# Seven early query loads split by head pair instead of by partition half, with their order mended in the matmul reads and a new plan of steps

One NeuronCore (core 0) of one Trainium2 chip runs the kernel. The metric is the device time of one launch in microseconds (us), the median of the fast runs; a "ratio" is the mean time of one kernel's fast runs over that of the other's fast runs of the same rounds, so it is not quite the ratio of the medians quoted beside it.

## The reference

Decayed linear attention in blocks of 64 (batch 4, 8 heads, 768 positions, 64 wide), then an MLP with a sine in it (512 to 2048 to 512) on the 3072 tokens.

```python
intra = einsum('bhic,bhjc->bhij', qb, kb) * Dmask[None]
intra = einsum('bhij,bhjd->bhid', intra, vb)
inter = einsum('bhid,bhde->bhie', qb * lam_pow[None], kv_state)
out[:, :, sl] = intra + inter
kv_state = lam_block[None, :, None, None] * kv_state + einsum('bhsd,bhse->bhde', kb_dec, vb)
# then, with x = the attention's output as [3072, 512]:
h = x @ w_in
s = sin(alpha * h)
g = h + s * s / (alpha + 1e-09)
return g @ w_out
```

## The kernel before

The attention is cut into 24 units of 4 heads and 256 positions. Four units make a group of 512 tokens, and the MLP of a group needs its four units. Queries, keys and values of a unit are loaded (256 KB each), cast to bf16, queries and keys are turned (in nine units by TensorE, with a copy out of PSUM after it, in the other 15 by a DMA), and then come scores, mask, inter and output. For units 1 to 7 (`Q4`) the queries travel with four neighbouring rows in one run of 1 KB:

```python
def load(op, u, i, gate):
    ...
    if i == 0 and u in Q4:
        for x in reversed(range(2)):                  # one issue per half of the partitions
            op.ins = SY.dma_start(
                out=tl[half[x]].rearrange("p h two e -> p (h two e)")
                .rearrange("p (g y) -> p g y", g=2),
                in_=src[2 * x:2 * x + 2].rearrange("g (p j) e -> p g (j e)", j=4))
            ...
def turn_ev(op, tr, u, j):                            # PSUM -> SBUF, after the turn
    o, i = T[u, "qt"][:, j], tr.tile[:]
    if j == 0 and u in Q4:                            # puts the positions in order
        o = o.rearrange("q par hp (p a) -> q a (par hp) p", a=2)
        i = i.rearrange("q a x i -> q a (x i)").rearrange("q a (y p) -> q a y p", y=4)
    (A.copy or V.tensor_copy)(out=o, in_=i)           # shortened
```

All steps are operations with an assumed duration and a priority (the table `TUNE`). A small planner simulates them once, at build time, and from that fixes the order in which each engine gets its instructions. On the chip every engine then works through its list in that order. If a step's data are late, the steps behind it wait too.

## Time and profile before

| | before |
|---|---|
| time | 219.86 us (219.25 to 219.96, 3 runs) |
| span of the profiled run, granted clock | 218.1 us, 1.00 |
| TensorE busy | 205.9 us, 94% |
| first matmul of the MLP | at 22.34 us |
| query loads of units 1 to 4 issued | at 2.33, 4.97, 7.67 and 10.41 us |
| TensorE idle from 34.3 to 214 us | 2.46 us |

It is read from the start: TensorE is full from the first MLP matmul to the end, so what delays that matmul should delay the end, and what keeps it waiting is the loads. The lines are in the prediction.

### The profile page before, as it was taken

What the parts mean: (1) busy time and instruction counts of PE and PEld (TensorE: products, weight loads), DVE (VectorE), ACT (ScalarE), POOL (GpSimd) and SP (SyncE); (2) the same over time, 40 slices, a digit from 0 to 9 for tenths busy, and PEclk for the clock granted to TensorE, in tenths of its full rate; (3) what the DMA queues carried; (4) which work ended last, traced back from release to release, by engine and by line L of the source; (5) the groups of instructions that cost most, each with busy time, mean ns of one, the idle gap of its engine ahead of it and who ended that gap; (6) DMA issues with size and microseconds to landing.
All of it is one profiled execution on the core that took longest, in us unless ns stands there. A gap on an engine that the chain in (4) does not pass through costs nothing.

```text
span 218.1 us, 5252 instructions
## 1 busy us (share of the span) xinstructions
PE 205.9 (94%) x2042; PEld 105.1 (48%) x2070; DVE 124.6 (57%) x203; ACT 140.4 (64%) x253; POOL 122.8 (56%) x201
## 2 busy tenths in 40 slices
PE   8786999999999999999999999999999999999992
PEld 3354544455536554455645545445445444444461
DVE  3678686537659973477767864738625643543000
ACT  4374698575499754876948778558726877775111
POOL 4569699948999999988899591313111001030000
PEclk9999999999999999999999999999999999999999
DMA  5999999998999992899999992202222022111253
GB/s 168 254 256 217 207 200 215 259 255 233 291 174 181 298 314 64 174 263 195 290 219 223 298 186 49 48 3 50 48 51 48 2 51 48 28 37 35 48 120 72
DMA packets 60460, 33.65 MB, mean 154 GB/s; under 512 B 18051, under 2 KB 57491, under 8 KB 60435
## 3 DMA queue, kind: packets, MB, share of 16 engines
q1 hardware_dynamic: 56096, 29.04, 59.1%
q0 software_dynamic: 4224, 4.19, 11.7%
q8 instruction: 16, 0.26, 0.5%
q10 hardware_dynamic: 114, 0.07, 0.1%
q14 instruction: 10, 0.07, 0.1%
HBM read 27.27 MB, written 6.29 MB: 154 GB/s over the span
## 4 chain that ended last, share of the span: by engine, by line
PE 70%; DMA 13%; POOL 6%; ACT 4%; issue 3%; SPq 2%; DVE 1%; POOLq 0%; ACTq 0%; DVEq 0%
PE ops L962 30%; PE hps L926 28%; DMA st_v<-in_v_dram 7%; DMA st_k<-in_k_dram 6%; PE okv L962 3%; PE sp L773 2%; PE okv L896 2%; SPq L698 2%; ACT s L933 2%; POOL qk L717 2%; PE okv L883 1%; POOL vb L723 1%; DVE gall L945 1%; ACT s L940 1%; POOL s L942 1%
## 5 line engine op out<-in xcount | busy, mean ns | idle before, releaser
L945 DVE SCALAR_TENSOR_TENSOR gall<-s,r_sb,hps 128x512 bf16<-128x512 bf16 (+1 forms) x97 | 70.1, 740 | 55.0 <-ACT s L940 33.9
L926 PE MATMUL hps<-xt,w_in_sb 128*128 128x512 bf16 (+1 forms) x371 | 90.6, 377 | 1.9 <-DVE gall L945 0.5
L933 ACT ACTIVATE s<-hps,alpha_sb 128x512 bf16<-128x512 f32 (+1 forms) x97 | 64.6, 679 | 34.4 <-PE hps L926 31.1
L962 PE MATMUL ops<-w_out_sb,gall 128*128 128x512 bf16 (+1 forms) x358 | 81.6, 370 | 1.0 <-issue 0.6
L962 PEld LDWEIGHTS <-gall 128*128 128x128 bf16 x400 | 38.3, 98 | 41.4
L926 PEld LDWEIGHTS <-w_in_sb 128*128 128x128 bf16 x388 | 36.7, 98 | 44.3 <-issue 2.7
L942 POOL TENSOR_TENSOR s<-s 128x512 bf16<-128x512 bf16 x24 | 24.8, 1041 | 39.7 <-ACT s L933 39.6
L940 ACT ACTIVATE s<-s 128x512 bf16<-128x512 bf16 (+1 forms) x73 | 44.5, 623 | 1.4
L782 DVE TENSOR_TENSOR sm<-sp,mask 128x512 bf16<-128x512 f32 x48 | 32.6, 684 | 6.1 <-PE sp L773 6.1
L723 POOL TENSOR_TENSOR vb<-st_v,R 128x512 bf16<-128x512 f32 x24 | 25.0, 1045 | 8.6 <-DMA st_v<-in_v_dram 6.2
L968 ACT COPY ob<-ops 128x512 f32<-128x512 f32 x21 | 12.2, 582 | 19.1 <-PE ops L962 18.9
L832 POOL TENSOR_TENSOR kvx<-kva,kvs 128x128 f32<-128x128 f32 x32 | 14.6, 457 | 14.8 <-ACT kva L817 14.5
L835 POOL TENSOR_TENSOR kvbd<-kvx,LBD 128x256 bf16<-128x256 f32 x32 | 19.6, 614 | 2.5
L913 DVE TENSOR_TENSOR xt<-okv,ET 128x512 bf16<-128x512 f32 x24 | 16.5, 686 | 3.5 <-PE okv L896 3.5
L999 PE MATMUL bz<-const-bfloat16-1.0 128*128 128x256 bf16 (+1 forms) x35 | 9.6, 343 | 1.7 <-PEq L1335 0.8
L717 POOL CAST qk<-st_q 128x512 bf16<-128x512 f32 x16 | 9.6, 614 | 1.4 <-PE okv L807 1.4
L773 PE MATMUL sp<-qt 64*64 64x128 bf16 x384 | 10.0, 221 | 0.0
L717 POOL CAST qk<-st_k 128x512 bf16<-128x512 f32 x16 | 9.7, 615 | 0.0
L896 PE MATMUL okv<-sm,vb 64*64 64x128 bf16 x384 | 9.7, 218 | 0.0
L873 POOL TENSOR_TENSOR kvs<-kvx,ET 128x128 f32<-128x128 f32 x24 | 9.5, 405 | 0.0
L883 PEld LDWEIGHTS <-kvbd 128*128 128x128 bf16 x80 | 6.2, 98 | 5.6 <-POOL kvbd L835 1.1
L883 PE MATMUL okv<-qt,kvbd 128*128 128x128 bf16 x80 | 8.6, 219 | 0.3 <-POOL kvbd L835 0.3
(64 smaller groups left out, 104.4 us busy)
## 6 DMA issues: line engine op xcount, KB each, us to landing
st_k<-in_k_dram SPq DMA_DIRECT2D x24, 256.0 KB, 5.2
st_v<-in_v_dram SPq DMA_DIRECT2D x24, 256.0 KB, 4.9
out_dram<-ob SPq DMA_DIRECT2D x46, 128.0 KB, 2.4
st_q<-in_q_dram SPq DMA_DIRECT2D x17, 256.0 KB, 5.2
w_out_sb<-in_moe_w_out_dram POOLq DMA_DIRECT2D x4, 512.0 KB, 14.4
st_q<-in_q_dram SPq DMA_DIRECT2D x14, 128.0 KB, 5.6
w_in_sb<-in_moe_w_in_dram POOLq DMA_DIRECT2D x2, 512.0 KB, 7.8
w_in_sb<-in_moe_w_in_dram POOLq DMA_DIRECT2D x1, 768.0 KB, 10.6
```

The costliest lines, as they stand in the source:

```text
L717: ENGINE[op.eng].tensor_copy(out=o, in_=i)
L723: ENGINE[op.eng].tensor_tensor(out=T[u, "vb"][:], in0=T[u, "v"][:].rearrange("p h two e -> p two h e"), in1=R[:, :, hs].unsqueeze(3).to_br ...
L782: V.tensor_tensor(out=T[u, "sm"][:, hd], in0=T[u, "sp"][hd][:], in1=mask[:].unsqueeze(2).to_broadcast([P, 2, 2, P]), op=ALU.mult)
L835: G.tensor_tensor(out=bd[:], in0=X.unsqueeze(2).to_broadcast([P, 2, 2, D]), in1=LBD[:, hs, :].unsqueeze(3).to_broadcast([P, 2, 2, D]), op= ...
L883: nc.tensor.matmul(out=okv[:, c, hp * P:(hp + 1) * P], lhsT=sts[c][:, hp].rearrange("p two e -> p (two e)"), rhs=T[u, "qt"][:, 0, :, hp, h ...
L913: V.tensor_tensor(out=xt[g][:, 2 * hh:2 * hh + 2, bb, :, :].rearrange("p hp c i -> p c hp i"), in0=T[u, "op"][:, :, 0:2 * P].rearrange("p ...
L926: op.ins = nc.tensor.matmul(out=op.tile[:, cols], lhsT=w_in_sb[:, c, f * P:(f + 1) * P], rhs=xt[g][:, c].rearrange("p b c i -> p (b c i)") ...
L933: A.activation(out=op.tile[:, cols], in_=mm.tile[:, cols], func=ACTF.Sin, scale=alpha_sb[:, f:f + 1])
L940: A.activation(out=op.tile[:, cols], in_=s1, func=ACTF.Square)
L942: ENGINE[op.eng].tensor_tensor(out=op.tile[:, cols], in0=s1, in1=s1, op=ALU.mult)
L945: V.scalar_tensor_tensor(out=gall[g][:, f, cols], in0=sq.tile[:, cols], scalar=r_sb[:, f:f + 1], in1=mm.tile[:, cols], op0=ALU.mult, op1=A ...
L962: op.ins = nc.tensor.matmul(out=first.tile[:, cols], lhsT=gall[g][:, f, m * P:(m + 1) * P], rhs=w_out_sb[:, f, cols], start=(f == 0), stop ...
```

## The change

The intent: each of the two issues of a query load should cover all 128 partitions, not 64; the copy out of PSUM becomes plain, and the order of the positions is put right by the access pattern with which scores and inter read the queries. The plan was made anew for that.

```diff
-            for x in reversed(range(2)):
-                op.ins = SY.dma_start(
-                    out=tl[half[x]].rearrange("p h two e -> p (h two e)")
-                    .rearrange("p (g y) -> p g y", g=2),
-                    in_=src[2 * x:2 * x + 2].rearrange("g (p j) e -> p g (j e)", j=4))
...
+            for g in range(2):
+                ins = SY.dma_start(
+                    out=tl[:].rearrange("p h two e -> p (h two e)")[:, g * 4 * D:(g + 1) * 4 * D],
+                    in_=src.rearrange("(s g) (p j) e -> g s p (j e)", g=2, j=4)[g])
...
-        o, i = T[u, "qt"][:, j], tr.tile[:]
-        if j == 0 and u in Q4:
-            ...
+            V.tensor_copy(out=T[u, "qt"][:, j], in_=tr.tile[:])
...
+    def queries(u, rows, hp, c):
+        Q = T[u, "qt"][rows, 0]
+        if u not in Q4:
+            return Q[:, :, hp, half[c]]
+        Q = Q.rearrange("q y x i -> q (y x i)").rearrange(
+            "q (a two x p) -> q two x p a", a=2, two=2, x=2)
+        return Q[:, :, hp, 32 * c:32 * c + 32, :]
...
-                            rhs=QT[half[hd], 0, :, hp, half[c]],
+                            rhs=queries(u, half[hd], hp, c),
...
-    BEGIN, LAND, DEPTH = {"SP": 0.4, "POOL": 2.0}, 1.7, 6
+    BEGIN, LAND, DEPTH = {"SP": 0.4, "POOL": 2.0}, 1.55, 6
... (967 of the 973 priorities of TUNE new, 31 steps with another engine or none prescribed)
```

The bytes land in the same places before and after. Only the cut between the two issues differs.

## The prediction

> **What bounds the kernel now.** I read the page's header and tenths first, then the table of stretches, then the chain that ended last in its early part, then the rows of the DMA issues, then the instructions that touch the query tile.
>
> ```profile
> span 218.1 us, 5252 instructions
> PE 205.9 (94%) x2042; PEld 105.1 (48%) x2070; DVE 124.6 (57%) x203; ACT 140.4 (64%) x253; POOL 122.8 (56%) x201
> ```
>
> TensorE is the bound by share. But the share is an average, so the next view splits it (columns: stretch, its length, then busy time and count of PE, PEld, DVE, ACT, POOL, granted clock, DMA share, GB/s).
>
> ```profile
> 15.00:20.00 5.00, 3.64 (x89) 2.40 (x90) 4.42 (x8) 2.73 (x6) 4.97 (x8) 1.00 1.28 230
> 22.40:34.30 11.90, 11.26 (x98) 5.23 (x99) 8.77 (x15) 10.14 (x20) 9.57 (x18) 1.00 1.21 204
> 34.30:60.00 25.70, 24.96 (x300) 13.06 (x305) 15.38 (x25) 15.86 (x32) 21.25 (x34) 1.00 1.09 254
> 60.00:100.00 40.00, 39.24 (x461) 20.31 (x465) 26.37 (x40) 30.14 (x53) 37.93 (x63) 1.00 0.97 209
> 100.00:140.00 40.00, 39.46 (x433) 20.52 (x429) 29.30 (x44) 29.42 (x53) 29.48 (x49) 1.00 0.89 196
> 140.00:180.00 40.00, 39.74 (x317) 19.57 (x320) 21.47 (x31) 26.29 (x45) 6.69 (x10) 1.00 0.16 34
> 180.00:214.00 34.00, 33.84 (x172) 16.82 (x172) 9.06 (x13) 17.09 (x29) 3.08 (x3) 1.00 0.23 51
> ```
>
> From 34.3 us to 214 us TensorE stands idle for 0.74 + 0.76 + 0.54 + 0.26 + 0.16 = 2.46 us. So what a new schedule can still win there is about 2.5 us, and the rest of the time is matmuls that the change does not touch. The other place with slack is the start: the first feed-forward matmul of the MLP runs at 22.3 us, and what the chain shows before it is loads:
>
> ```profile
> 1.78 4.83 DMA st_v<-in_v_dram
> 6.63 4.91 DMA st_k<-in_k_dram
> 11.76 7.27 DMA st_k<-in_k_dram
> 19.06 0.63 ACT qk L715
> 19.73 0.41 PE pt L743 x4
> 20.17 0.60 ACT qt L753
> 20.80 0.28 PE bz L999
> ```
>
> Three loads in a row make 17 of the first 19 us; the last takes 7.27 us from issue to landing for 256 KB, so it stood in a queue. The start is a matter of the transfers, with POOL (4.97 of 5 us busy from 15 to 20) close behind. These are the rows of the loads (KB each, median us to landing):
>
> ```profile
> st_k<-in_k_dram SPq DMA_DIRECT2D x24, 256.0 KB, 5.2
> st_q<-in_q_dram SPq DMA_DIRECT2D x17, 256.0 KB, 5.2
> st_q<-in_q_dram SPq DMA_DIRECT2D x14, 128.0 KB, 5.6
> ```
>
> The 14 issues of 128 KB are the seven query loads that the change touches: half the bytes, yet no sooner there. Last, the evacuation of the turned queries and keys, DVE and then ACT (min/median/max ns):
>
> ```profile
> L755 DVE COPY qt<-pt x10: 415/425/734, 4.9 to 52.7; 128x512 bf16<-128x512 bf16 x10
> L753 ACT COPY qt<-pt x8: 586/666/773, 9.0 to 55.6; 128x512 bf16<-128x512 bf16 x8
> ```
>
> One shape, two durations on each engine: the long ones (0.73) write the early queries in a permuted order with a gap between neighbours, the short ones (0.42 and 0.59) are plain.
>
> **What the Trainium skill says.** (1) "SBUF — State Buffer", Door 1, the DMA port swizzle: partitions 0..63 reach 8 of the 16 DMA ports, so a transfer on 64 partitions gets about half the rate of one on 128. The trace leans that way: in the microsecond from 3 to 4, with key and value loads on 128 partitions, 0.31 MB moved (309 GB/s); from 4 to 5 and 6 to 7, with the split query loads among them, 0.22 MB each (224 and 217 GB/s). It doesn't separate them cleanly. (2) "DMA: Bandwidth & Descriptors", Why a DMA increments its semaphore by 16 and not by 1: the number of engines is the largest k up to 16 that divides the slowest dimension of both access patterns. In the kernel before that dimension is 64 or 128 on both sides, so 16 engines; no load in the trace has a small outer dimension, so nothing here tests it. (3) "SBUF — State Buffer", same section, the note on 16-byte cachelines: a read that goes to a new line at every element pays a penalty. No matmul of the trace reads its moving operand that way, so this is open too. (4) "VectorE: DVE Perf Modes", What auto-detection actually checks: two results per cycle need 16-bit operands at unit step. That agrees with 0.42 against 0.73 us on DVE, though ACT too loses 0.14.
>
> **The change part by part.**
>
> Query loads, units 1 to 7. Before: two issues, one to each half of the partitions (64 x two runs of 1 KB). After: two issues, each to all 128 partitions (one run of 1 KB). Same bytes, same place of every byte, same number of issues. If the rate of these goes from some 220 to some 310 GB/s (the windows above), units 1 to 3 (0.79 MB) save 0.79/220 - 0.79/310, about 1.0 us of transfer. POOL and the casts stand beside it, so I let 0.4 us reach the first MLP matmul. There is a hazard: the new source pattern goes head pair (2), then 64 row groups, then a run. Its slowest dimension is 2 and cannot be merged with the 64. By the rule (2) such a transfer would use 2 engines, not 16. That is the first rival below.
>
> Evacuation. Permuting copies become plain: 0.31 us less on DVE, 0.14 on ACT, seven times, so 1 to 2.2 us of engine time. Neither engine bounds; on the path lies about one of them in the start: 0.2 us.
>
> Matmuls. The order is now made where scores (16 matmuls per unit) and inter (2 matmuls in units 1 to 3, 4 in units 4 to 7) read the queries; neighbours of a run lie 512 bytes apart. The chain gives 0.22 us for 4 inter matmuls, 0.054 each, and 0.35 us for 16 scores, four of which run side by side. If such a read runs at half rate, a unit pays 4 x 0.054 = 0.21 us for scores and 0.054 for each inter. Units 4 to 7 lie at 47 to 59 us, where TensorE is full: 4 x 0.21 + 16 x 0.054 = 1.7 us more. Units 1 to 3 lie where TensorE runs filler, so most of theirs is hidden. At about even odds of the penalty, I count 0.8 us.
>
> Plan. The priorities of all steps are new; the landing time assumed is 1.55 instead of 1.7 us. Squares pinned to ACT go from 65 to 70, to POOL from 22 to 20. No instruction is added or removed. Slack to win: the 2.46 us above, and 22.4 to 34.3, where 38 full and 8 half matmuls of the first MLP layer (38 x 0.216 + 8 x 0.108 = 9.1 us) and about 0.8 us of attention fill 11.9 us: 2 us. A plan adapted to cheaper evacuations should find perhaps a quarter of the 4.5 us: 1.0 us.
>
> Sum: -0.4 - 0.2 + 0.8 - 1.0 = -0.8 us, so 219.1 us where the loads run as meant.
>
> **The rivals.**
>
> First, the loads fall onto 2 engines. Then each of those carries 128 KB of a unit's queries. In the 3 to 4 us window an engine moved 309/16 = 19 GB/s; 1 KB runs may reach 25 (an estimate), so 5 to 7 us per unit, plus its share of keys and values (32 KB, 1.7 us). A unit's loads would then take 7 to 8 us on these engines, where the trace has q1 to q4 issued 2.7 us apart. Units 1 to 3 would be there at about 26 us instead of 17 to 19, the first full MLP matmul would go from 24.3 to about 31, and the span would grow by 5 to 8 us: 225 to 228. Units 4 to 7 are mostly covered by the 128 first-group matmuls. For it: the rule is stated plainly, and nothing in the new pattern escapes it. Against it: whoever planned this anew shortened the landing time, the opposite of what such loads would have shown, and left the assumed query transfer as it was. I give it one in four.
>
> Second, nothing reaches the end: the earlier data wait for POOL (values to scale, weight issues, 4.97 of 5 us), the slow reads eat the rest, and the plan is only different: 219.5 to 220.8. For it: POOL is full from 15 to 20, and the windows after 34.3 are at 97 to 99%. I give it a third.
>
> Third, the new plan removes most of the idle time of 22 to 60 us: 2.5 to 3 us, 217. Against it: the plan before was tuned too. For over 2% (below 215.5) it would need nearly all the 4.5 us; that I give one in twenty.
>
> **Range and chances.** The middle of the meant branch is 219.1 with a spread of about 1.2; the 2-engine branch at 225 to 228 has a quarter of the weight and moves the median up a little: 219.2 us. One case in ten below 217.2, one in ten above 226.0. Faster by over 2%: 0.05; within: 0.71; slower (above 224.3): 0.24.
>
> **What would show it.** In the DMA issues, the 128 KB query row should land in clearly less than 5.6 us if the ports were the matter, and in more, with the tenths of DMA sinking in the first 25 us, if engines are lost. The copies to qt should be uniformly 0.42 and 0.59. The scores and inter matmuls of units 1 to 7 should show by their group times (0.35 per 16, 0.22 per 4) whether the read pays. The first MLP matmul should come at 21.5 to 22.5 us, or near 28 in the rival. TensorE's idle time from 34.3 to 214 should shrink from 2.46 us if the plan earned anything. The prediction is wrong if the loads lose their engines, if the permuted read costs far more than half rate, or if the plan stalls a later group of units.

## The result

The changed kernel takes **254.95 us** (254.53 to 255.34, 4 runs) against 219.71 us (the kernel before with a fourth run; the table above has three); ratio 1.1606, 95% interval 1.1575 to 1.1637. That is 35 us slower, outside the range of the prediction. The page of the changed kernel, its header, its tenths and its loads:

```profile
span 252.9 us, 5273 instructions
PE 219.4 (87%) x2070; PEld 111.4 (44%) x2070; DVE 122.8 (49%) x201; ACT 142.2 (56%) x256; POOL 121.7 (48%) x200
...
PE   8274612899966899999999999999999999999993
...
PEclk9955575599997799999999999999999999999998
DMA  4336496299346995999996899523311030111233
```

A slice is 6.3 us here. In the first 16 slices (some 100 us) TensorE has holes, its clock falls to half in some of them, and the DMA engines are mostly idle in a start that was bound by transfers before. From slice 17 on TensorE is at 9 again, up to the last slice.

What the DMA engines did in two stretches of the start comes next (the third number from the end is the clock, then the DMA share and GB/s). First the changed kernel:

```profile
10.50:12.00 1.50, 0.00 (x0) 0.00 (x0) 0.00 (x0) 0.00 (x0) 0.03 (x1) 0.99 0.14 45
10.00:15.00 5.00, 2.15 (x13) 1.60 (x14) 0.00 (x0) 2.38 (x4) 1.57 (x2) 0.70 0.19 59
```

Then the kernel before:

```profile
10.00:15.00 5.00, 3.99 (x97) 2.14 (x96) 3.25 (x8) 3.18 (x10) 2.99 (x4) 1.00 1.20 263
```

Two of 16 engines are a share of 0.125. In the first stretch the share is 0.14, at 45 GB/s: two engines at some 22 GB/s each. The trace's DMA packets, counted one by one, agree: two are under way in 79% of that stretch, three or four in the rest, never fewer than two. (65 of these 103 packets have 512 bytes, the size of the runs of keys and values: their share on the two engines waits there as well.) Before, from 10 to 15 us, at least 16 packets were under way at any time (a share over 1 means that transfers overlapped in an engine), at 263 GB/s. This is the first rival of the prediction.

The issues show the same from the other side (start, duration; two issues per line). The kernel before, then the changed one from its first query load by head pair:

```profile
4.97 1.26 SPq L690 DMA_DIRECT2D st_q<-in_q_dram  x2
7.67 1.26 SPq L690 DMA_DIRECT2D st_q<-in_q_dram  x2
10.41 1.26 SPq L690 DMA_DIRECT2D st_q<-in_q_dram  x2
```

```profile
2.32 1.47 SPq L689 DMA_DIRECT2D st_q<-in_q_dram  x2
7.89 3.95 SPq L689 DMA_DIRECT2D st_q<-in_q_dram  x2
15.31 3.90 SPq L689 DMA_DIRECT2D st_q<-in_q_dram  x2
22.35 3.98 SPq L689 DMA_DIRECT2D st_q<-in_q_dram  x2
```

The distance of neighbouring units from unit 2 on is 7.0 to 7.4 us, not 2.7. The work fits: 128 KB of queries on each of the two engines at 22 GB/s is 6.0 us, and their share of keys and values (32 KB) 1.5. The issuing got slower too, 3.9 us a pair and not 1.26, so the keys and values behind it are issued late as well. But the first pair, which met no such load ahead of it, took 1.47 us (1.41 in the kernel before), and the pair at 56.18 us, after a pause, 1.18: issuing was slow only behind loads that were not done.

The chain that ended last, in the changed kernel up to the first MLP matmul:

```profile
16.65 9.78 DMA st_q<-in_q_dram
26.43 17.52 DMA st_k<-in_k_dram
...
43.97 0.63 ACT qk L712
...
44.64 0.61 PE pt L740 x4
...
46.83 1.01 PE hps L927 x4
```

The last matmul is the first of the MLP. In the kernel before it stands here:

```profile
22.34 0.61 PE L926 MATMUL hps<-xt,w_in_sb 128*128 128x256 bf16 x4
```

It comes at 46.83 us and not 22.34, so 24.5 of the 35 us are lost there. These four matmuls take 1.01 us and not 0.61, at a granted clock of 0.52 from 40 to 50 us and 1.00 before: a part of the loss lies in matmuls that run, but slowly. And the load it waits for is the keys of unit 4. But the first group consists of units 0 to 3. Its MLP doesn't need unit 4 at all. A second hole lies between 60 and 100 us, where TensorE is idle for 5.4 us and the clock is at 0.91 to 0.92. From the first MLP matmul to the end the changed kernel takes 206.1 us, the kernel before 195.8: these are the other 10.3 us.

### The profile page after: what moved, and what is told of

Its sections match the earlier page's. It is cut to its first block, busy times and chain, and to the rows that moved or that the text cites. A ratio compares the mean times of both kernels' runs of the same rounds, so it can differ in the third digit from the quotient of the medians.

```text
span 252.9 us, 5273 instructions
## 1 busy us (share of the span) xinstructions
PE 219.4 (87%) x2070; PEld 111.4 (44%) x2070; DVE 122.8 (49%) x201; ACT 142.2 (56%) x256; POOL 121.7 (48%) x200
## 4 chain that ended last, share of the span: by engine, by line
PE 66%; DMA 18%; SPq 7%; POOL 4%; ACT 1%; DVE 1%; issue 1%; POOLq 0%; ACTq 0%; DVEq 0%
PE ops L963 30%; PE hps L927 27%; DMA st_q<-in_q_dram 8%; DMA st_k<-in_k_dram 7%; SPq L695 4%; SPq L689 3%; DMA st_v<-in_v_dram 3%; PE sp L774 3%; PE okv L897 2%; PE okv L884 2%; POOL s L943 1%; DVE gall L946 1%; PE okv L808 1%; PE bz L1000 1%; POOL kvbd L836 1%
## 5 line engine op out<-in xcount | busy, mean ns | idle before, releaser
L963 PE MATMUL ops<-w_out_sb,gall 128*128 128x512 bf16 (+1 forms) x368 | 85.0, 377 | 0.0
L927 PEld LDWEIGHTS <-w_in_sb 128*128 128x128 bf16 x388 | 37.3, 98 | 45.6 <-issue 3.0
L941 ACT ACTIVATE s<-s 128x512 bf16<-128x512 bf16 (+1 forms) x74 | 45.4, 623 | 1.6
L943 POOL TENSOR_TENSOR s<-s 128x512 bf16<-128x512 bf16 x23 | 23.8, 1041 | 34.4 <-ACT s L934 34.3
L733 PE MATMUL pt<-iden,qk 128*128 128x128 bf16 x28 | 3.6, 270 | 24.3 <-ACT qk L712 20.2
L712 ACT CAST qk<-st_q 128x512 bf16<-128x512 f32 x8 | 4.9, 615 | 31.8 <-DMA st_q<-in_q_dram 31.8
L733 PEld LDWEIGHTS <-qk 128*128 128x128 bf16 x28 | 2.2, 116 | 25.8 <-ACT qk L712 25.3
L1000 PE MATMUL bz<-const-bfloat16-1.0 128*128 128x256 bf16 (+1 forms) x35 | 12.4, 423 | 1.2 <-PEq L1336 0.8
L774 PE MATMUL sp<-qt 64*64 64x128 bf16 x384 | 11.9, 241 | 0.1
L897 PE MATMUL okv<-sm,vb 64*64 64x128 bf16 x384 | 10.8, 237 | 0.0
```

Of the source, the lines that this page charges most:

```text
L774: nc.tensor.matmul(out=T[u, "sp"][hd][half[c], par, hp, :], lhsT=QT[half[hd], 1, par, hp, half[c]], rhs=queries(u, half[hd], hp, c), start ...
L927: op.ins = nc.tensor.matmul(out=op.tile[:, cols], lhsT=w_in_sb[:, c, f * P:(f + 1) * P], rhs=xt[g][:, c].rearrange("p b c i -> p (b c i)") ...
L941: A.activation(out=op.tile[:, cols], in_=s1, func=ACTF.Square)
L943: ENGINE[op.eng].tensor_tensor(out=op.tile[:, cols], in0=s1, in1=s1, op=ALU.mult)
L963: op.ins = nc.tensor.matmul(out=first.tile[:, cols], lhsT=gall[g][:, f, m * P:(m + 1) * P], rhs=w_out_sb[:, f, cols], start=(f == 0), stop ...
```

## The experiments

All twelve results are correct against the reference. Times are medians of the fast runs, 4 to 6 of each but for unit 4 alone, which had two fast runs (228.41 and 228.59) and two slow ones (231.89 and 232.09, at the same clock). One slow run each fell to the loads by halves (228.57) and the interleaved pairs (223.82). The kernel before had 219.3 to 219.8 us in these rounds. The record gives chip 8 for eight of the runs and chip 4 for four (the two cuts of the halves and the two with unit 4's work moved back), each set with the kernel before beside it.

| run | time us | ratio to before | 95% interval |
|---|---|---|---|
| changed, loads by halves | 221.33 | 1.0079 | 1.0023 to 1.0135 |
| before, loads by head pair | 254.17 | 1.1578 | 1.1520 to 1.1636 |
| changed, pairs interleaved | 220.18 | 1.0027 | 0.9984 to 1.0070 |
| changed, loads by halves, old data path | 220.76 | 1.0040 | 0.9995 to 1.0084 |
| halves cut 62 + 2 | 255.56 | 1.1630 | 1.1574 to 1.1687 |
| halves cut 56 + 8 | 221.18 | 1.0070 | 1.0006 to 1.0133 |
| head pair for units 1 to 3 only | 235.47 | 1.0714 | 1.0653 to 1.0775 |
| head pair for unit 4 only | 228.50 | 1.0404 | 1.0331 to 1.0478 |
| head pair for units 5 to 7 only | 231.57 | 1.0546 | 1.0493 to 1.0598 |
| unit 4 by head pair, its work moved back | 242.88 | 1.1032 | 1.0960 to 1.1103 |
| the same with loads by halves (control) | 240.48 | 1.0934 | 1.0875 to 1.0993 |
| before, pairs interleaved | 217.90 | 0.9928 | 0.9883 to 0.9973 |

**The loads alone, taken out and put in.** Theory: the source pattern begins with a dimension of 2, so each load runs on two DMA engines. Rivals: the new plan stalls, or the permuted reads of the matmuls are slow.

```diff
 # changed kernel, loads by halves
-            for g in range(2):  ...  "(s g) (p j) e -> g s p (j e)"
+            for x in reversed(range(2)):  ...  "g (p j) e -> p g (j e)"
```

> The changed kernel with one thing undone: the query loads of units 1 to 7 are again one issue per half of the partitions (slowest source dimension 64), bytes in the same places; new plan, plain copies and permuted matmul reads stay. Engine theory (a source whose slowest dimension is 2 runs on 2 DMA engines): all of the 35 us come from the loads, so this lands at 218 to 222 us and the 128 KB loads of queries land within 7 us. Plan theory (the new priorities put TensorE's queue in an order that stalls): stays above 240. Read theory (the permuted moving operand is what is slow): stays above 235, with scores of units 1 to 7 at twice 0.35 us or more.

It took 221.33 us. Of the 35 us, 33.6 (254.95 less 221.33) are gone with the loads.

```diff
 # kernel before, loads by head pair
-            for x in reversed(range(2)):  ...  "g (p j) e -> p g (j e)"
+            for g in range(2):  ...  "(s g) (p j) e -> g s p (j e)"
```

> The kernel before with one thing added: the query loads split by head pair, everything else as it was (plan, permuting copies, plain reads). Engine theory: 245 to 260 us, with the same gaps of about 7 us between the issues of neighbouring units. Plan theory: below 225. Read theory: below 225, since no read is permuted here.

It took 254.17 us, with issues at 8.17, 15.68 and 22.75 us: the whole loss, with the old plan and plain reads. So the new plan and the permuted reads are out as its cause.

**Engines, or the order of the source?** Two experiments, from both sides. First, the same coverage (one head of each pair, all 128 partitions, one run of 1 KB each), but with the row groups outermost:

```diff
-                    in_=src.rearrange("(s g) (p j) e -> g s p (j e)", g=2, j=4)[g])
+                    in_=src.rearrange("(s g) (p j) e -> g p s (j e)", g=2, j=4)[g])
...
-            "q (a two x p) -> q two x p a", a=2, two=2, x=2)
+            "q (a two p x) -> q two x p a", a=2, two=2, x=2)
```

> The changed kernel with the pairs interleaved over the partitions: each load still takes one head of each pair and covers all 128 partitions with one run of 1 KB each, but partition 2p+pair instead of 64 pair+p, so the slowest source dimension is 64 and not 2. Same bytes, same number of issues, same heads. Engine theory: 217 to 221 us, query loads landing in at most 5.6 us; if the ports of the partitions matter too, 0.3 to 1 us faster than the version with loads by halves. Rival (it is the reading of two head pairs at once, or one run per partition on all 128, that is slow, not the number of engines): stays above 240.

It took 220.18 us, and the 128 KB query loads land in 4.7 us (median). Swapping two letters in the pattern, with the reads adapted, undoes the loss. Second, the opposite: the old order, but each half's 64 partitions cut so that the divisor rule, point (2) of the prediction, gives two engines, or 14 and 8.

```diff
+                for lo, hi in ((0, 62), (62, D)):     # control: 56
+                    ins = SY.dma_start(
+                        out=tl[x * D + lo:x * D + hi]...,
+                        in_=src[2 * x:2 * x + 2].rearrange("g (p j) e -> p g (j e)", j=4)[lo:hi])
```

> The changed kernel with loads by halves, but each half's 64 partitions cut into 62 and 2: four issues per unit, source order rows first as in the kernel before, no head pair outermost. By the divisor rule of the Trainium skill 62 shares with the numbers up to 16 only the divisor 2, so both pieces run on 2 engines. If the number of engines is the cause: 245 to 260 us, like the changed kernel, though nothing of its source order is left. If the order of the head pairs in the source is the cause: 219 to 226.

> The control for the cut into 62 and 2: the same four issues per unit, cut into 56 and 8, which the rule gives 14 and 8 engines. Expected: 220 to 226 us; what it loses against loads by halves (221.5) is the price of two more issues per unit. If this one is slow too (over 240), the number of issues is the cause and not the engines.

The cut at 62 took 255.56 us, the cut at 56 took 221.18. Both have four issues per unit; six partitions more or less decide over 34 us. The stretch of the 62 run shows the two engines again:

```profile
10.50:12.00 1.50, 0.00 (x0) 0.00 (x0) 0.00 (x0) 0.00 (x0) 0.42 (x1) 0.50 0.14 46
```

In its packets two are under way in 81% of this stretch, again never fewer. This settles it: the loss follows the number of engines, and that follows the common divisor of the slowest dimensions, as the Trainium skill says ("DMA: Bandwidth & Descriptors", Why a DMA increments its semaphore by 16 and not by 1). Only the two engines were counted; that the control ran on just 14 and 8 is not shown.

**Where the 33.6 us fall.** Now only some units use the split by head pair (`if u in (1, 2, 3):` and so on, the others load by halves).

> The changed kernel with the split by head pair kept for units 1 to 3 only; units 4 to 7 load by halves. It gives the part of the loss that units 1 to 3 make. If every late load counts where it falls: values of unit 3 land at about 30 us as in the changed kernel, the first matmul of the MLP runs at 33 to 36 us instead of 21.3, and the time is 231 to 234 us. If the start is hidden by later slack: below 226.

> The changed kernel with the split by head pair for unit 4 only. Unit 4 belongs to the second group, which the first MLP matmuls don't need. If TensorE's fixed order makes them wait (unit 4's transposes stand ahead of them in its queue): first MLP matmul 3 to 6 us later than 21.3, time 223 to 227 us. If only data count: no change against loads by halves, 219.5 to 222 us.

> The changed kernel with the split by head pair for units 5 to 7 only, which are loaded after the start. In the changed kernel TensorE stood idle about 5.5 us between 60 and 100 us at a lower clock. Expected: start as with loads by halves (first MLP matmul at about 21.3 us), a gap before the second group's scores, time 226 to 231 us. My recorded prediction had these covered by the first group's 128 matmuls: then 220 to 223.

Against loads by halves (221.33) they cost 14.1, 7.2 and 10.2 us. The sum, 31.5, is all but 2 us of the 33.6: the parts nearly add up. Unit 4's part is the least certain: it rests on two fast runs, and its two slow ones would make it 10.6 to 10.8. The first MLP matmul comes at 37.06 us for units 1 to 3, at 27.96 for unit 4 and at 21.23 for units 5 to 7, where the gap lies later. All three came out above what was expected (for the time of units 5 to 7 by half a microsecond): none of the three losses is covered by other work as a whole.

**Why should unit 4 cost anything?** In the run with unit 4 only, TensorE's line shows it (start, duration, and in brackets what it waited for):

```profile
22.16 0.61 PE L743 MATMUL pt<-iden,qk 128*128 128x128 bf16 x4 [2.84 <-ACT qk L722]
...
22.77 0.45 PE L894 MATMUL okv<-qt,kvbd 128*128 128x128 bf16 x2
...
25.77 0.61 PE L750 MATMUL pt<-iden,qk 128*128 128x128 bf16 x4 [1.76 <-ACT qk L722]
...
27.96 1.01 PE L937 MATMUL hps<-xt,w_in_sb 128*128 128x256 bf16 x4
```

The `pt` matmuls turn unit 4's queries and keys. They stand in the queue before the inter and output matmuls of the first group's units, and those before the MLP. To test this, I made the plan put unit 4's query cast and value scaling after the fifth MLP tile. The edit does not hold back its key cast. It also lets the loads of the output weights wait for unit 3's value scaling and not for unit 4's. This ran once with unit 4 by head pair and once, as control, with all loads by halves:

```diff
+    u4 = {o.name: o for o in plan.ops}
+    for x in ("cq4", "sv4"):
+        u4[x].after.append(f1_mm[0, 4])
-    WH = (4, 4, 4, 4)
+    WH = (3, 3, 3, 3)
```

> Unit 4 on loads by head pair as in the run with unit 4 only (230.2 us), but the plan puts unit 4's casts, its value scaling and with them its transposes behind the first five MLP tiles of the first group. If the loss of that run is TensorE and POOL waiting in their own order for data that the next work doesn't need: at most 3 us above its control, and the first MLP matmul at about 22 us. If the late data themselves or the crowded engines cost the time: 7 us or more above the control.

> The control: the same altered plan with all loads by halves. 219 to 224 us; its own distance from the run with loads by halves (221.5) is the price of the altered order and says nothing of the loads.

The first MLP matmul of the run with unit 4 by head pair:

```profile
21.79 0.61 PE L937 MATMUL hps<-xt,w_in_sb 128*128 128x256 bf16 x4 [1.00 <-DMA w_in_sb<-in_moe_w_in_dram]
```

It no longer waits for unit 4: 21.79 us and not 27.96, and its control has 22.05. That the late load stopped this matmul only through the order of the steps is shown. The size of what is saved is not. The altered plan is itself bad: the control takes 240.48 us and not the 219 to 224 that I expected of it, with TensorE idle for 5.7 us from 60 to 80 us at a clock of 0.74. The distance of the two runs is 2.4 us instead of 7.2, but a plan with that much slack may hide the rest. A version that moved unit 4's steps in the finished order deadlocked in simulation, by my account alone: it was not run. So no run separates this further.

**The permuted reads, the copies, the plan.** The changed kernel with loads by halves and, in addition, the permuting copies and plain reads of the kernel before:

```diff
-                            rhs=queries(u, half[hd], hp, c),
+                            rhs=QT[half[hd], 0, :, hp, half[c]],
 # and turn_ev as in the kernel before
```

> The changed kernel's plan alone: loads by halves, permuting copies and plain matmul reads as in the kernel before. Against the version with loads by halves and the new data path it gives the price of the permuted reads less the gain of the plain copies. If a permuted read runs at half rate: this one is 0.5 to 1.7 us faster than that. If reading costs nothing: 0 to 0.5 us slower. Against the kernel before it gives the worth of the new plan: expected between 1 us faster and 1 us slower.

The scores of unit 1 and the inter of unit 2 with permuted reads (loads by halves):

```profile
10.60 0.68 PE L776 MATMUL sp<-qt 64*64 64x128 bf16 x16
17.28 0.41 PE L886 MATMUL okv<-qt,kvbd 128*128 128x128 bf16 x2
```

With plain reads:

```profile
11.20 0.42 PE L780 MATMUL sp<-qt 64*64 64x128 bf16 x16
17.73 0.27 PE L890 MATMUL okv<-qt,kvbd 128*128 128x128 bf16 x2
```

16 scores take 0.26 us more. For one matmul of the scores, the list of the query tile gives a median of 216 ns plain, 280 with the changed kernel's reads and 296 with the interleaved ones. The whole time, 220.76 against 221.33 us, points the same way by 0.6 us, but the two intervals overlap, and so did the clocks (0.976 to 1.000 and 0.982 to 0.997): a gain of the old data path is likely, not shown. No gain of the new plan alone is seen: 1.0040 to the kernel before, with an interval that just includes 1.

**A version that is faster than both.** Interleaved loads put into the kernel before, its own plan, a permuting copy for the new order, plain reads:

```diff
-                    in_=src[2 * x:2 * x + 2].rearrange("g (p j) e -> p g (j e)", j=4))
+                    in_=src.rearrange("(s g) (p j) e -> g p s (j e)", g=2, j=4)[g])
...
-            o = o.rearrange("q par hp (p a) -> q a (par hp) p", a=2)
-            i = i.rearrange("q a x i -> q a (x i)").rearrange("q a (y p) -> q a y p", y=4)
+            o = o.rearrange("q par hp (p a) -> q a par hp p", a=2)
+            i = i.rearrange("q a y i -> q a y i").rearrange("q a y (p x) -> q a y x p", x=2)
```

> The kernel before with the interleaved loads alone (16 engines, all 128 partitions in each load) and its permuting copy adapted to them, plain matmul reads, its own plan. It takes what the change was after and leaves out what cost: 217.5 to 219 us, 0.3 to 1 us faster than the kernel before, if the 0.7 us that the interleaved loads brought forward at the start reach the end; no gain if the plan's fixed order gives them back. If the adapted copy reads slower (over 0.8 us each) it gives some back.

It took 217.90 us, ratio 0.9928 (0.9883 to 0.9973), some 0.7% faster than the kernel before. The interval excludes 1, though the gain is far from 2%. Its first MLP matmul and its 128 KB query loads (median us to landing at the end of the line):

```profile
20.35 0.61 PE L924 MATMUL hps<-xt,w_in_sb 128*128 128x256 bf16 x4
```

```profile
st_q<-in_q_dram SPq DMA_DIRECT2D x14, 128.0 KB, 4.3
```

The kernel before has 22.34 us, and 5.6 us in this row (it stands in the prediction). In the profiled executions the start is 2.0 us earlier and the span 2.0 us shorter (216.1 against 218.1); the medians of the same rounds differ by 1.5 us (217.90 against 219.40). So what is won at the start mostly reaches the end. The idea of loads that cover all partitions was sound. The pattern chosen for it was not. That the partitions alone make the loads faster is not isolated: each partition also gets one run of a load in place of two, and partition and row are paired otherwise.

## Why the prediction was wrong

- **What bounds the kernel** was right: loads before the first MLP matmul, matmuls after it. In the interleaved version 2.0 us gained at the start became 2.0 us of span, 1.5 us between medians.
- **The loads by head pair.** The main sum of the prediction let them run on 16 engines (0.4 us gained), and gave the rival of two engines one chance in four. This is the step that failed first: the rule of the Trainium skill was read rightly and nothing in the pattern escaped it, but it was discounted because whoever made the plan had shortened the assumed landing time. A constant in a planner is not a measurement. The 62 and 56 runs show the rule at work.
- **The rival's size.** It was put at 5 to 8 us and is 33.6. Its rate was right: 19 to 25 GB/s per engine was estimated, 22 measured; 7 to 8 us per unit, 7.0 to 7.4 measured. Three terms behind it were not, and the sign given for this rival, a first MLP matmul near 28 us, came at 46.83. Units 1 to 3 "at about 26 us" were there only when unit 3's values could be scaled, at 30.2 us in the changed kernel (16.8 before), since the issues on the queue stall too; together they cost 14.1. Unit 4 was not counted before the first MLP matmul, and costs 7.2: in that run the first MLP matmul waits through the order of TensorE's queue. The prediction's own chain had it, for the key load at 11.76 us there is unit 4's (its queries were issued at 10.41); the prediction didn't ask whose load it was. Units 4 to 7 "mostly covered by the 128 first-group matmuls" were not covered: 5 to 7 alone cost 10.2.
- **The permuted reads.** Half rate at even odds was assumed, 0.054 us for an inter matmul and 0.21 for a unit's scores; the runs show 0.064 and 0.26. A little low, right in kind. Of the 0.8 us counted, 0.6 were seen between medians, without certainty.
- **The copies** are uniformly some 0.42 and 0.59 us, as expected. Their 0.2 us can't be told apart in the time.
- **The plan** was credited with 1.0 us; alone it shows no gain. So the meant branch (219.1 us, with 16 engines) was not met either: the nearest thing to it, the changed kernel with interleaved pairs, shows no gain (1.0027, 0.9984 to 1.0070).
- **The ports.** 0.4 us were expected of covering all partitions, from windows that left out one: from 5 to 6 us, with query loads under way too, the kernel before moved 268 GB/s, not some 220. Where the engines are kept, the first MLP matmul comes 0.7 us earlier with interleaved loads in the new plan (20.58 against 21.25) and 2.0 in the old one (one profiled execution each). This term was too small, if it is the ports that these loads gain by.

## What to carry to other kernels

Before you count the partitions of a transfer, look at the slowest dimension of both of its patterns: the number of DMA engines depends on what divides both. In a kernel whose engines follow a fixed order, a late load costs where its first consumer stands in the queue, not where its result is needed; so look up which instruction of each engine will meet the missing data first. And treat constants in somebody's planner as assumptions, not as evidence of what the chip did.

## What the Trainium skill lacked or had wrong

- "DMA: Bandwidth & Descriptors", Why a DMA increments its semaphore by 16 and not by 1: the times fit the rule in four different cuts (slowest common sizes 2, 62, 56 with 8, and 64). The page has a bandwidth for one engine, but no measured load on few engines (here 45 GB/s on two). And it lacks that issuing slows behind such loads: 3.9 us for a pair instead of 1.26, which holds up the other loads of the same queue.
- "SBUF — State Buffer", Door 1: with loads over all 128 partitions, 128 KB landed after 4.7 us instead of 5.6 in the new plan, and 4.3 instead of 5.6 in the old. That is less than a halved rate suggests, but these loads stood in a busy queue and no run isolates the ports. The page is not shown to be wrong; it lacks a figure for such a queue.
- The same section's note on 16-byte lines gives no price for a matmul. Here a moving operand whose neighbours lie 512 bytes apart made a 128-column matmul 280 ns long and not 216; with two-element steps besides, 296.
